# High parts of the weights on GpSimd, high parts of x and the rounding constant on ScalarE: a fused kernel of attention, token mixing and gated attention

## The chip, the cores and the metric

The kernel runs as one launch on one core of a Trainium2 chip. The metric is the device time in microseconds. The kernel before took 553.32 us (median of three runs, 553.31 to 554.25).

## The reference

Inputs are float32, apart from the token-mixing weights (`w_theta`, `w_tok_r`, `w_tok_i`, `w_ch`), which the kernel receives as float64. The data passes through three stages, 4 batches, 576 positions, 512 channels:

```python
# 1: attention, 8 heads of 64: heads 0-3 see the last 32 positions, heads 4-7 every 32nd one before
scores = scale * q @ k.T; scores = where(mask, scores, -1e9)
attn = softmax(scores); x = attn @ v                       # (B, 576, 512)
# 2: token mixing
theta = x @ w_theta
yr = einsum('ts,bsd->btd', w_tok_r, x * cos(theta))
yi = einsum('ts,bsd->btd', w_tok_i, x * sin(theta))
u = x + yr + yi
x = u + maximum(u @ w_ch, 0)
# 3: 4 experts of causal attention (q, k, v, o projections per expert), a gate picks 2 for each position
logits = x @ w_gate; out = sum over the best 2 experts of softmax gate * expert(x)
```

## The kernel before, in words

**Two halves of each number.** Every matmul of stage 2 and most of stage 3 is done on numbers split in two: a high part, rounded by writing to the type fp32r, and a low part, the number less its high part. `mm3` (lines 264 to 268) then issues three matmuls: high by high (L266), high by low (L267), low by high (L268).

**Weights.** `load64` (l. 122) brings a float64 weight in 34 pieces of 128 partitions: 8 of `w_theta` (wth, 256 columns), 18 of the token weights (wtk, 288 columns), 8 of `w_ch` (wch, 256 columns). Each piece takes a DMA of the raw words into one of eight slots (four in buffer X[1], four in X[3]; L135, issued by SyncE), a cast of the top bits on ScalarE (L139), a shift-and-or on VectorE that makes a float32 (L140), and then `split_w`: the high part by an ACTIVATE on ScalarE (L102), the low part by a subtraction on VectorE (L104; L106 for wth, where a scale comes in). A slot is free for the next raw piece once L139 and L140 of the piece in it are done.

**Stage 1** (`attn_pair`, l. 173) goes by pair of heads: scores (s, L189), maximum and exponential, sum and reciprocal (L215 to L217), the product p by it (L218: VectorE in batch 0, GpSimd in the others), the transpose of p on TensorE (tp, L221), the values (av) and a copy into X (L249, L251). The pairs of batch 1 run among the matmuls of stage 2 of batch 0: `next_pair` loads their q, k and v and calls `attn_pair`.

**Stage 2.** `split_act` (l. 254) splits x: the high part (L260) on VectorE for batch 0, on ScalarE (L258) for stage 2's output; the low part at L262. `theta` (l. 276) makes 5 tiles of theta in each of two halves of 256 columns, adds the constant MAGIC (L289, VectorE, which rounds to whole turns), takes the difference (L290), its absolute value (L291, ScalarE), and `sines` the cosine (L303, with a bias read from a tile) and the sine (L304), whose table ScalarE has to load first. `rotate` multiplies x (transposed by TensorE to xn, L312) by both (L322; L328 and L329 for the short last tile), and splits the product z: high part L332 or L334, low part L336. `tokens` runs y (L266 to L268) and adds it into X (L351), splits the sum u (L361), and `channels` makes g from it.

**The order of the work.** No order is written out: the program is built with a scheduler that simulates a timeline and decides the order of the instructions on each engine, so that a changed duration or engine moves other instructions. `issue_after` holds back a few of them. TensorE's accumulator of `th` and of the first `y` is the same pair of buffers (`acc`), so y starts when the last reader of a th tile, L290, has let it go.

Of the kernel before, what the change touches and what calls it, by code (L numbers as in the profile page):

```python
# [12 lines left out]
F32 = mybir.dt.float32  # L13
# [5 lines left out]
AF = mybir.ActivationFunctionType  # L19
ALU = mybir.AluOpType  # L20
# [3 lines left out]
B, S, DM, HD, NE = 4, 576, 512, 64, 4  # L24
# [17 lines left out]
MAGIC = 12582912.0  # L42
# [5 lines left out]
def fused_kernel(ctx: ExitStack, tc: tile.TileContext, ql, kl, vl, qs, ks, vs, wth, wtk, wch, wqk, wvg, wo, out):  # L48
    nc = tc.nc

    def f(ap):
        return ap.bitcast(F32)

    const = ctx.enter_context(tc.tile_pool(name="const", bufs=1))
# [44 lines left out]

    pha = ph1.enter_context(ExitStack())  # L100
    def split_w(hi, lo, st, scale=1.0, eng=nc.gpsimd):
        nc.scalar.activation(hi, st, AF.Copy, scale=scale)  # L102
        if scale == 1.0:
            eng.tensor_tensor(lo, st, f(hi), op=ALU.subtract)  # L104
        else:
            nc.vector.scalar_tensor_tensor(lo, st, scale, f(hi), op0=ALU.mult, op1=ALU.subtract)  # L106

    def load_split(pool, spool, src, kt, n, name):
        hi = pool.tile([128, kt, n], F32R, name=f"{name}_hi")
        lo = pool.tile([128, kt, n], F32R, name=f"{name}_lo")  # L110
        for c in range(kt):
            st = spool.tile([128, 512], F32, tag="stage", name=f"{name}_st{c}")
            nc.sync.dma_start(st[:, :n], src[:, c, :])
            split_w(hi[:, c, :], lo[:, c, :], st[:, :n])
        return hi, lo
# [6 lines left out]
    def load64(dst, src, kt, n0, n1, scale=1.0, late=False):  # L122

        hi, lo = dst
        n = n1 - n0
        for c in range(kt):  # L130
            place = X[3] if late or len(pieces) % 2 else X[1]
            raw = place.bitcast(U16)[:, len(pieces) // (1 if late else 2) % 4, :4 * n]
            pieces.append(c)
            st = X[2][:, c % 4, HALF:HALF + n]
            nc.sync.dma_start(raw[:, :4 * n - 1], src[:, c, n0:n1].bitcast(U16)[:, 1:])  # L135
            mid = raw.bitcast(U32).rearrange("p (n t) -> p n t", t=2)[:, :, 0]
            top = raw.bitcast(BF16).rearrange("p (n t) -> p n t", t=4)[:, :, 2]
            head = X[2][:, c % 4, :n]
            got = nc.scalar.copy(head.bitcast(F16).rearrange("p (n t) -> p n t", t=2)[:, :, 1], top)  # L139
            nc.vector.scalar_tensor_tensor(st.bitcast(U32), mid, 13, head.bitcast(U32), op0=ALU.logical_shift_right,  # L140
                                           op1=ALU.bitwise_or)
            split_w(hi[:, c, n0:n1], lo[:, c, n0:n1], st, scale, nc.vector)
        return got.ins
# [110 lines left out]
    def split_act(x, name):  # L254
        hi = act.tile([128, S], F32R, tag="ahi", name=f"{name}_hi")
        lo = act.tile([128, S], F32R, tag="alo", name=f"{name}_lo")
        if len(xsplit) == B:
            nc.scalar.copy(hi, x)  # L258
        else:
            nc.vector.tensor_copy(hi, x)  # L260
        eng = nc.vector if not xsplit or len(xsplit) == B and name.endswith(("0", "2")) else nc.gpsimd
        halved[name] = eng.tensor_tensor(lo, x, f(hi), op=ALU.subtract).ins  # L262
        return hi, lo

    def mm3(ps, ahi, alo, bhi, blo, first, last):
        nc.tensor.matmul(ps, ahi, bhi, start=first, stop=False)  # L266
        nc.tensor.matmul(ps, ahi, blo, start=False, stop=False)  # L267
        return nc.tensor.matmul(ps, alo, bhi, start=False, stop=last)  # L268

    def split_x(b):  # L270
        return [split_act(X[b][:, c, :], f"x{len(xsplit)}_{b}_{c}") for c in range(4)]

    sins, turns = {}, {}
    xsplit, trig, z = {}, {}, {}

    def theta(b, h):
        if h == 0:
            xsplit[b] = split_x(b)
        xs = xsplit[b]
        d0 = 256 * h  # L280
        for t in range(NT):
            w, t0 = TW[t], 128 * t
            th = ps1.tile([128, 512], F32, tag="s" if b == 0 and t % 2 else "acc", bufs=2, name=f"th_{b}_{h}_{t}")
            for c in range(4):
                turned = mm3(th[:w, :256], xs[c][0][:, t0:t0 + w], xs[c][1][:, t0:t0 + w],
                             wth_hi[:, c, d0:d0 + 256], wth_lo[:, c, d0:d0 + 256], c == 0, c == 3)
            cs = rp.tile([128, 2, 256], F32, tag="cs", name=f"cs_{b}_{h}_{t}")
            r = cs[:w, 1, :]
            nc.vector.tensor_scalar_add(r, th[:w, :256], MAGIC)  # L289
            nc.vector.scalar_tensor_tensor(r, r, MAGIC, th[:w, :256], op0=ALU.subtract, op1=ALU.subtract)  # L290
            last = nc.scalar.activation(cs[:w, 0, :], r, AF.Abs)  # L291
            trig[h, t] = cs
            if b == 0:
                sines(b, h, range(t, t + 1))
        if b > 0:
            with tc.issue_after(last.ins):
                sines(b, h, range(NT))
        return turned.ins

    def sines(b, h, tiles):  # L300
        for t in tiles:
            w, cs = TW[t], trig[h, t]
            nc.scalar.activation(cs[:w, 0, :], cs[:w, 0, :], AF.Sin, bias=halfpi[:w], scale=-TWO_PI)  # L303
            sins[b, h] = nc.scalar.activation(cs[:w, 1, :], cs[:w, 1, :], AF.Sin, scale=-TWO_PI).ins  # L304
# [69 lines left out]

    halfpi = const.tile([128, 1], F32, name="halfpi")
    nc.gpsimd.memset(halfpi, math.pi / 2)
    spark = const.tile([128, 1], F32, name="spark")

    nc.vector.memset(X[2][:, :, :HALF], 0.0)
# [26 lines left out]

    for b in range(B):
        theta(b, 0)
        if b > 0:
            next_pair(b, 0)  # L410
# [5 lines left out]
        if b > 0:  # L416
            next_pair(b, 1)
        turned = theta(b, 1)
        if b > 0:
            next_pair(b, 2)  # L420
# [372 lines left out]
```

## Time and profile before

| | |
|---|---|
| time, median of 3 | 553.32 us |
| the profiled execution | 551.97 us, span 550.1 us |
| mean granted TensorE clock | 0.986 of full speed |
| TensorE busy | 526.1 us of 550.1 |
| VectorE, ScalarE, GpSimd busy | 398.7, 316.1, 188.3 us |
| HBM traffic | 67 GB/s over the span |

The span is 1.9 us shorter than the execution's time. The profile's times run from the span's start. The stage in which the float64 weights arrive and batch 0 is worked through is the first 100 us; what follows is a repeated pattern of the other batches and then the experts.

### The profile page before, as it was taken

What the parts mean: (1) busy time and instruction counts of PE and PEld (TensorE: products, weight loads), DVE (VectorE), ACT (ScalarE), POOL (GpSimd) and SP (SyncE); (2) the same over time, 40 slices, a digit from 0 to 9 for tenths busy, and PEclk for the clock granted to TensorE, in tenths of its full rate; (3) what the DMA queues carried; (4) which work ended last, traced back from release to release, by engine and by line L of the source; (5) the groups of instructions that cost most, each with busy time, mean ns of one, the idle gap of its engine ahead of it and who ended that gap; (6) DMA issues with size and microseconds to landing.
All of it is one profiled execution on the core that took longest, in us unless ns stands there. A gap on an engine that the chain in (4) does not pass through costs nothing.

```text
span 550.1 us, 12483 instructions
## 1 busy us (share of the span) xinstructions
PE 526.1 (96%) x4536; PEld 503.4 (91%) x4536; DVE 398.7 (72%) x1222; ACT 316.1 (57%) x904; POOL 188.3 (34%) x273
## 2 busy tenths in 40 slices
PE   6898999999999999999999999989999999999987
PEld 5788899999999999999999998879989999999987
DVE  5979997676855566765456443798988898888972
ACT  5978984426453171632236321585787768767872
POOL 1000013321742114541125533264446434625451
PEclk9959999999999999999999999999999999999999
DMA  8966253460202141000100111000001001100112
GB/s 289 321 191 255 82 162 109 167 198 1 91 23 67 33 133 33 24 24 1 58 0 2 29 31 40 1 1 2 1 12 66 14 1 45 44 2 11 35 44 87
DMA packets 20389, 37.53 MB, mean 68 GB/s; under 512 B 2904, under 2 KB 12296, under 8 KB 20328
## 3 DMA queue, kind: packets, MB, share of 16 engines
q1 hardware_dynamic: 20328, 36.73, 20.5%
q8 instruction: 36, 0.59, 0.4%
q14 instruction: 25, 0.20, 0.1%
HBM read 32.01 MB, written 4.72 MB: 67 GB/s over the span
## 4 chain that ended last, share of the span: by engine, by line
PE 72%; DVE 12%; ACT 8%; DMA 4%; issue 2%; POOL 2%; SPq 0%; POOLq 0%; DVEq 0%; ACTq 0%
PE y L266 7%; PE y L268 7%; PE y L267 7%; PE s L189 4%; PE av L244 4%; PE g L266 3%; PE g L268 3%; PE g L267 3%; PE tp L221 3%; PE th L266 3%; DVE nm L604 3%; PE th L268 3%; PE th L267 3%; ACT p L615 2%; PE tp L625 2%
## 5 line engine op out<-in xcount | busy, mean ns | idle before, releaser
L266 PE MATMUL y<-wtk_hi,zhi 128*128 128x288 f32 x288 | 86.4, 302 | 1.5 <-DVE cs L290 1.1
L267 PE MATMUL y<-wtk_lo,zhi 128*128 128x288 f32 x288 | 85.6, 298 | 0.0
L268 PE MATMUL y<-wtk_hi,zlo 128*128 128x288 f32 x288 | 85.1, 296 | 0.0
L218 POOL TENSOR_TENSOR p<-p,sm 128x288 f32<-128x288 f32 (+2 forms) x36 | 22.2, 623 | 157.4 <-PE y L268 72.2
L622 POOL TENSOR_SCALAR p<-p,sm,gt 128x256 f32<-128x256 f32 (+1 forms) x64 | 45.5, 714 | 51.9 <-DVE sm L620 34.9
L615 ACT ACTIVATE p<-s,nm 128x128 f32<-128x128 f32 (+2 forms) x96 | 49.6, 518 | 15.1 <-DVE nm L604 7.8
L266 PEld LDWEIGHTS y<-wtk_hi,zhi 128*128 128x128 f32 x288 | 53.9, 188 | 2.1 <-ACT wtk_hi L102 1.2
L267 PEld LDWEIGHTS y<-wtk_lo,zhi 128*128 128x128 f32 x288 | 54.1, 188 | 0.0
L268 PEld LDWEIGHTS y<-wtk_hi,zlo 128*128 128x128 f32 x288 | 54.0, 188 | 0.1
L336 POOL TENSOR_TENSOR zlo<-cs,zhi 128x512 fp32r<-128x512 f32 (+1 forms) x30 | 36.0, 1214 | 46.6 <-DVE zhi L332 41.1
L266 PE MATMUL th<-wth_hi,x_hi 128*128 128x256 f32 (+1 forms) x160 | 47.8, 300 | 0.5 <-ACT X L251 0.5
L604 DVE TENSOR_REDUCE nm<-s 128x1 f32<-128x128 f32 (+2 forms) x96 | 44.2, 468 | 5.3 <-PE s L602 4.4
L267 PE MATMUL th<-wth_lo,x_hi 128*128 128x256 f32 (+1 forms) x160 | 45.6, 286 | 0.0
L268 PE MATMUL th<-wth_hi,x_lo 128*128 128x256 f32 (+1 forms) x160 | 45.4, 288 | 0.0
L189 PE MATMUL s<-k,q 128*108 128x54 f32 (+2 forms) x320 | 40.9, 268 | 2.6 <-DMA k<-in_kl 1.8
L189 PEld LDWEIGHTS s<-k,q 128*108 128x108 f32 (+1 forms) x320 | 39.0, 190 | 3.7 <-DMA q<-in_ql 1.7
L266 PE MATMUL pq<-x_hi,wqk_hi 128*128 128x288 f32 x128 | 39.8, 311 | 1.0 <-DVE q L550 0.9
L262 POOL TENSOR_TENSOR x_lo<-X,x_hi 128x576 fp32r<-128x576 f32 x20 | 29.3, 1466 | 30.8 <-DVE x_hi L260 24.4
L266 PE MATMUL g<-u_hi,wch_hi 128*128 128x288 f32 x128 | 38.6, 302 | 0.0
L634 DVE TENSOR_TENSOR ptlo<-tp,pthi 128x128 fp32r<-128x128 f32 (+4 forms) x80 | 37.6, 478 | 1.1 <-ACT pthi L633 0.6
L267 PE MATMUL pq<-x_lo,wqk_hi 128*128 128x288 f32 x128 | 38.0, 297 | 0.0
L268 PE MATMUL g<-u_hi,wch_lo 128*128 128x288 f32 x128 | 37.8, 295 | 0.0
(173 smaller groups left out, 1676.6 us busy)
## 6 DMA issues: line engine op xcount, KB each, us to landing
X<-in_wtk SPq DMA_DIRECT2D x18, 287.8 KB
q<-in_qs SPq DMA_DIRECT2D x8, 594.0 KB
q<-in_ql SPq DMA_DIRECT2D x8, 576.0 KB
v<-in_vl SPq DMA_DIRECT2D x24, 144.0 KB
out_t<-X SPq DMA_DIRECT2D x20, 128.0 KB
k<-in_kl SPq DMA_DIRECT2D x8, 304.0 KB
k<-in_ks SPq DMA_DIRECT2D x8, 288.0 KB
X<-in_wth SPq DMA_DIRECT2D x8, 255.8 KB
```

The source lines that it names most:

```text
L189: nc.tensor.matmul(s[:rm, i * kw:i * kw + w], qt[:, j0 + i, :], kt[:, k0:k0 + w], start=False, stop=i == n - 1)
L218: (nc.vector if b == 0 else nc.gpsimd).tensor_tensor(tiles(p), tiles(p), each(sm), op=ALU.mult)
L244: nc.tensor.matmul(av[64 * h:64 * h + 64, c0:c0 + wi], vg[:w, i, h, :], pt[:w, i, h, :wi], start=True, stop=True)
L262: halved[name] = eng.tensor_tensor(lo, x, f(hi), op=ALU.subtract).ins
L266: nc.tensor.matmul(ps, ahi, bhi, start=first, stop=False)
L267: nc.tensor.matmul(ps, ahi, blo, start=False, stop=False)
L268: return nc.tensor.matmul(ps, alo, bhi, start=False, stop=last)
L336: halved[b, h] = eng.tensor_tensor(lo, zf, f(hi), op=ALU.subtract).ins
L604: nc.vector.tensor_reduce(nm[:w, t + ci:t + ci + 1], s[:w, :c1 - c0], axis=AX.X, op=ALU.max, negate=True)
L615: nc.scalar.activation(p[:w, c0:c1], scs[ci][:w, :c1 - c0], AF.Exp, bias=nm[:w, t:t + 1], scale=1.0, accum_out=acc)
L622: eng.tensor_scalar(p[:w, :kn], p[:w, :kn], sm[:w, t:t + 1], gt[:w, t, e:e + 1], op0=ALU.mult, op1=ALU.mult)
L634: nc.vector.tensor_tensor(dst(ptlo), src, f(dst(pthi)), op=ALU.subtract)
```

## The change

Three edits. In `split_w` the high part of the 34 float64 pieces is made by a TENSOR_SCALAR on GpSimd (L103), in place of ScalarE's ACTIVATE; other callers of `split_w` keep ScalarE. In `split_act` the four high parts of x of batch 0 are made by ScalarE instead of VectorE. In `theta`, for batch 0, the ten additions of MAGIC go from VectorE to ScalarE (L293, an Identity with a bias read from a new tile `magic`, which GpSimd fills once).

```diff
@@ split_w
-        nc.scalar.activation(hi, st, AF.Copy, scale=scale)
+        if eng is nc.vector:
+            nc.gpsimd.tensor_scalar(hi, st, scale, 1.0, op0=ALU.mult, op1=ALU.mult)
+        else:
+            nc.scalar.activation(hi, st, AF.Copy, scale=scale)
@@ split_act
-        if len(xsplit) == B:
+        if len(xsplit) in (0, B):
             nc.scalar.copy(hi, x)
         else:
             nc.vector.tensor_copy(hi, x)
@@ theta
-            nc.vector.tensor_scalar_add(r, th[:w, :256], MAGIC)
+            if b == 0:
+                nc.scalar.activation(r, th[:w, :256], AF.Identity, bias=magic[:w])
+            else:
+                nc.vector.tensor_scalar_add(r, th[:w, :256], MAGIC)
@@ constants
+    magic = const.tile([128, 1], F32, name="magic")
+    nc.gpsimd.memset(magic, MAGIC)
```

In the changed kernel the lines from L102 on stand 3 higher, and those behind L289 6 higher (L140 is L143, L104 is L107, L217 is L220, L290 is L296, L303 is L309, L336 is L342). The scheduler's order differs up to the second theta half of batch 1; from there on TensorE's order is the same.

SyncE's issues, around the loads of batch 1's first two pairs (`X` with the slots' numbers is a raw piece of wtk, `q_1_1` and `k_1_1` are the second pair's inputs). Before:

```order
L166 DMA v_1_0_2_987<-in_vl 96x384
L135 DMA X1_62<-in_wtk 128x1151
L135 DMA X3_64<-in_wtk 128x1151
L135 DMA X1_62<-in_wtk 128x1151
L135 DMA X3_64<-in_wtk 128x1151
L161 DMA q_1_1_1075<-in_ql 128x1152
```

And now:

```order
L169 DMA v_1_0_2_989<-in_vl 96x384
L164 DMA q_1_1_1077<-in_ql 128x1152
L165 DMA k_1_1_1078<-in_kl 128x608
L138 DMA X1_62<-in_wtk 128x1151
L138 DMA X3_64<-in_wtk 128x1151
L138 DMA X1_62<-in_wtk 128x1151
```

The ninth piece of wtk (the first `X1` row behind `v_1_0_2`) and those that follow it stand behind `q_1_1` and `k_1_1` now.

ScalarE's work up to the first sine of batch 0 (`cs_0_0_0` is the first tile of the first half, `cs_0_0_1` the second). Before:

```order
L139 CAST X2_63<-X3_64 128x288
L102 ACTIVATE wtk_hi_112<-X2_63 128x288 x2
L139 CAST X2_63<-X1_62 128x288
L102 ACTIVATE wtk_hi_112<-X2_63 128x288 x3
L291 ACTIVATE cs_0_0_0_630<-cs_0_0_0_630 128x256
L303 ACT_TABLE_LOAD
```

And now:

```order
L293 ACTIVATE cs_0_0_0_632<-th_0_0_0_619,magic_108 128x256
L293 ACTIVATE cs_0_0_1_651<-th_0_0_1_638,magic_108 128x256
L293 ACTIVATE cs_0_0_2_670<-th_0_0_2_657,magic_108 128x256
L142 CAST X2_63<-X1_62 128x288
L297 ACTIVATE cs_0_0_0_632<-cs_0_0_0_632 128x256
L293 ACTIVATE cs_0_0_3_689<-th_0_0_3_676,magic_108 128x256
L297 ACTIVATE cs_0_0_1_651<-cs_0_0_1_651 128x256
L309 ACT_TABLE_LOAD
```

The cast of the ninth piece of wtk stands ahead of the table load in both. Behind it stood three high parts and one absolute value; now there are two absolute values and one addition of MAGIC.

VectorE's work ahead of the first reciprocal of batch 1's attention (`sm_1_0_0`). Before:

```order
L140 SCALAR_TENSOR_TENSOR X2_63<-X3_64,X2_63 128x256
L104 TENSOR_TENSOR wtk_lo_113<-X2_63,wtk_hi_112 128x288
L104 TENSOR_TENSOR wch_lo_115<-X2_63,wch_hi_114 128x256
L361 TENSOR_TENSOR u_0_0_lo_1288<-X0_61,u_0_0_hi_1287 128x288
L361 TENSOR_TENSOR u_0_1_lo_1292<-X0_61,u_0_1_hi_1291 128x288
L211 TENSOR_TENSOR p_1_0_2_1039<-s_1_0_2_1032,mx_1_0_2_1037 128x288
L217 RECIPROCAL sm_1_0_0_995<-sm_1_0_0_995 128x3
L216 TENSOR_SCALAR sm_1_0_1_1017<-sm_1_0_1_1017 128x3
```

And now:

```order
L143 SCALAR_TENSOR_TENSOR X2_63<-X3_64,X2_63 128x256
L342 TENSOR_TENSOR zlo_0_1_4_931<-cs_0_1_4_889,zhi_0_1_4_930 128x256
L218 TENSOR_REDUCE sm_1_0_1_1019<-p_1_0_1_1020 128x3
L367 TENSOR_TENSOR u_0_0_lo_1290<-X0_61,u_0_0_hi_1289 128x288
L367 TENSOR_TENSOR u_0_1_lo_1294<-X0_61,u_0_1_hi_1293 128x288
L107 TENSOR_TENSOR wch_lo_117<-X2_63,wch_hi_116 128x256
L143 SCALAR_TENSOR_TENSOR X2_63<-X3_64,X2_63 128x256
L220 RECIPROCAL sm_1_0_0_997<-sm_1_0_0_997 128x3
```

The last `L143` row ahead of the reciprocal is the fourth piece of wch; before, that reciprocal came behind the second. From the release of the first accumulator by `L290` (tile `cs_0_1_2`) to this reciprocal VectorE had 44 instructions and has 47, one of them 288 columns wide more and two of 256.

## Rows read from the trace of the kernel before

**Rows 1.** Page part 1, busy time and share of the span by engine:

```profile
PE 526.1 (96%) x4536; PEld 503.4 (91%) x4536; DVE 398.7 (72%) x1222; ACT 316.1 (57%) x904; POOL 188.3 (34%) x273
```

**Rows 2.** Timeline of PE, its four stops (start, duration, instruction, idle before):

```profile
36.06 0.58 PE L266 MATMUL th<-wth_hi,x_hi 128*128 128x256 f32 x1 [0.49 <-ACT X L251]
...
54.11 0.41 PE L312 MATMUL xn<-ident,X 128*128 128x128 f32 x2 [1.65 <-DVE cs L329]
...
57.93 0.37 PE L266 MATMUL y<-wtk_hi,zhi 128*128 128x288 f32 x1 [1.10 <-DVE cs L290]
...
76.78 0.43 PE L221 MATMUL tp<-ident,p 128*96 128x128 f32 x2 [0.71 <-POOL p L218]
```

**Rows 3.** Windows: stretch, length, busy PE, PEld, DVE, ACT, POOL, clock, DMA, GB/s:

```profile
24.00:28.00 4.00, 2.11 (x25) 1.27 (x23) 4.00 (x16) 4.00 (x25) 0.00 (x0) 0.80 0.68 227
28.00:36.00 8.00, 6.97 (x84) 5.71 (x83) 5.29 (x18) 5.28 (x17) 0.00 (x0) 0.50 0.50 150
...
40.00:44.00 4.00, 4.00 (x36) 4.00 (x35) 3.72 (x11) 2.49 (x8) 0.00 (x0) 1.00 1.07 339
52.00:58.00 6.00, 3.25 (x27) 2.63 (x24) 5.94 (x16) 5.25 (x16) 0.00 (x0) 1.00 0.08 13
58.00:77.00 19.00, 18.29 (x142) 17.81 (x143) 18.94 (x51) 16.97 (x49) 1.40 (x1) 1.00 0.48 148
```

**Rows 4.** Groups by form on ACT: count, busy and mean ns, idle before:

```profile
L102 ACT ACTIVATE wtk_hi<-X 128x288 fp32r<-128x288 f32 x18 | 7.4, 434 | 0.2 <-DVE X L140 0.2
L258 ACT CAST x_hi<-X 128x576 fp32r<-128x576 f32 x16 | 10.0, 672 | 0.2 <-PE th L267 0.2
L303 ACT ACTIVATE cs<-cs,halfpi 128x256 f32<-128x256 f32 x32 | 16.0, 499 | 0.1
```

**Rows 5.** Groups by form on DVE:

```profile
L289 DVE TENSOR_SCALAR cs<-th 128x256 f32<-128x256 f32 x32 | 13.3, 420 | 7.2 <-PE th L268 6.7 <-POOL zlo L336 0.4
L260 DVE CAST x_hi<-X 128x576 fp32r<-128x576 f32 x16 | 9.1, 580 | 2.5 <-ACT X L251 2.3
```

**Rows 6.** Group by form on POOL:

```profile
L555 POOL TENSOR_SCALAR k<-k 64x288 fp32r<-64x288 f32 x32 | 14.5, 453 | 16.2 <-ACT k L553 14.5
```

**Rows 7.** Timeline of DVE: its first wtk piece, and two back-to-back low parts:

```profile
37.21 1.56 DVE L140 SCALAR_TENSOR_TENSOR X<-X,X 128x288 uint32<-128x288 uint32 x4
...
60.99 0.81 DVE L104 TENSOR_TENSOR wtk_lo<-X,wtk_hi 128x288 fp32r<-128x288 f32 x2
```

**Rows 8.** Timeline of ACT from the ninth wtk piece to the first sine:

```profile
42.84 0.53 ACT L139 CAST X<-X 128x288 f16<-128x288 bf16 x1 [1.51 <-DMA X<-in_wtk]
43.23 1.11 ACT L102 ACTIVATE wtk_hi<-X 128x288 fp32r<-128x288 f32 x3
...
46.43 0.40 ACT L304 ACTIVATE cs<-cs 128x256 f32<-128x256 f32 x1
```

**Rows 9.** Page part 6, DMA issues of SyncE, count and KB each:

```profile
q<-in_ql SPq DMA_DIRECT2D x8, 576.0 KB
...
k<-in_kl SPq DMA_DIRECT2D x8, 304.0 KB
```

**Rows 10.** Timeline of DVE, the first reciprocal of batch 1:

```profile
74.99 0.16 DVE L217 RECIPROCAL sm<-sm 128x3 f32<-128x3 f32 x1
```

**Rows 11.** Timeline of DVE and POOL where both work, and where DVE works alone:

```profile
75.12 0.41 DVE L140 SCALAR_TENSOR_TENSOR X<-X,X 128x256 uint32<-128x256 uint32 x1
...
77.86 0.67 POOL L218 TENSOR_TENSOR p<-p,sm 128x288 f32<-128x288 f32 x1 [1.13 <-DVE sm L217]
77.98 0.83 DVE L140 SCALAR_TENSOR_TENSOR X<-X,X 128x256 uint32<-128x256 uint32 x1
...
403.04 0.33 DVE L622 TENSOR_SCALAR p<-p,sm,gt 128x128 f32<-128x128 f32 x1
...
518.65 0.43 POOL L555 TENSOR_SCALAR k<-k 64x288 fp32r<-64x288 f32 x1 [0.32 <-ACT k L553]
518.65 0.51 DVE L622 TENSOR_SCALAR p<-p,sm,gt 128x128 f32<-128x128 f32 x1
```

## The prediction

> **What bounds the kernel now.** I read the page's shares first, then TensorE's timeline for its stops, then a table by stretch, and last the rows of the engines named in the stops. TensorE is busy for 96% of the span [rows 1], so the change can only gain what TensorE still waits for, and it can lose whatever makes it wait anew. All three edits touch the weights, x and theta of batch 0, so they lie in the first 77 us. There TensorE stops four times for one of these engines [rows 2]: 0.49 us at 36.06 (for the last copy of attention on ScalarE), 1.65 at 54.11 and 1.10 at 57.93 (both for VectorE), 0.71 at 76.78 (for a product on GpSimd, whose reciprocal VectorE made at 74.99 [rows 10]). From 58 to 77 it runs otherwise without a gap, 18.29 of 19 us. So the later stops add up to some 3.5 us, the most that an edit in this stretch can return, apart from a slow clock: from 28 to 36 TensorE is granted 0.50 of its clock (1.2 GHz), from 40 on all of it (2.4 GHz) [rows 3].
>
> What the reader is to see in the table by stretch is VectorE: 5.94 of 6 us busy from 52 to 58, 18.94 of 19 from 58 to 77, 3.72 of 4 from 40 to 44 [rows 3]. From its first wtk piece at 37.21 [rows 7] to the reciprocal's end at 75.15 it works 36.6 of 37.9 us. It makes the sines' arguments, the low parts and the reciprocal in one queue. GpSimd is empty there, but for the product p that starts at 75.33 and is 1.40 us busy in the window. So relieving VectorE would pay, relieving ScalarE alone would not.
>
> **The change part by part.** Removed from VectorE: 4 x high parts at 0.580 and 10 additions at 0.420 [rows 5], with two of the ten shorter: about 6 us by these means. Back to back an instruction takes less than its own duration: two 288-wide low parts in 0.81 [rows 7], a pitch of 0.37 with the ramp taken off; in the same way I use 0.34 for 256 columns and 0.60 for 512. Removed from ScalarE: 34 high parts, 18 of them at 0.434 [rows 4]. Added to ScalarE: 4 casts of x at 0.672 and 10 additions, which I price by the form with a bias from a tile, 0.499, pitch 0.42 [rows 4]. Added to GpSimd: 34 TENSOR_SCALARs; the nearest row is 0.453 for 64 by 288 [rows 6]. That is 34 x 0.45 = 15.3 us on an engine with nothing else to do, in a chain that was cast, shift, high, low and still is: by throughput it costs nothing. Four terms follow in time.
>
> First, theta starts sooner. VectorE has its last p of attention behind fewer low parts of wth, about three of 0.34 less, and TensorE, at half clock, gives on most of that: 0.85, start 35.2.
>
> Second, the last x high part stands on ScalarE behind four wtk casts that it used to precede on VectorE, and its low part goes ahead of VectorE's first wtk piece: 37.21 becomes 38.0, a loss of 0.8 that eats what the first term gave.
>
> Third, the ninth wtk piece. In the order of SyncE's issues `q_1_1` and `k_1_1` now stand ahead of it: 576 + 304 KB [rows 9]. At 339 GB/s [rows 3] that is 2.6 us; I take 2.4, an estimate, since the ends of such loads run side by side. The queue is 0.85 earlier by the first term, so the piece lands 1.5 later than its 42.84 [rows 8], at 44.4; ScalarE already waits 1.51 for that DMA before, so nothing hides the delay. Behind it ScalarE had 1.11 us of high parts [rows 8] and one absolute value before the table load; now it has two absolute values and an addition. So the first sine's end, 46.83 before [rows 8], goes to about 47.9: 1.5 of the landing, less some 0.4 of the shorter queue. From there ScalarE's chain of five additions, absolute values and sines is the one that VectorE waits for, but VectorE has no additions any more. I get the first accumulator's release at 56.1, y at 56.2 instead of 57.93: 1.7 gained there.
>
> Fourth, from this release to the reciprocal. Before, that was 57.78 to 75.15, 17.4 us for 44 instructions; now there are 47, one of 288 columns and two of 256 more: 0.37 + 2 x 0.34 = 1.05, so 18.4. To this comes a price that no row shows in this form: 13 of the high parts (9 wtk, 4 wch) run on GpSimd beside VectorE's two-input instructions. At 77.98 an L140 took 0.83 where the same instruction took 0.41 at 75.12, and the GpSimd product began at 77.86: VectorE was held 0.42. The single-input TENSOR_SCALAR of GpSimd, which the new instruction is, went with 0.51 for an L622 against 0.33 undisturbed, a hold of 0.18 [rows 11]. The bounds are thus zero (GpSimd's instruction waits in place of VectorE's) and 13 x 0.45 = 5.9; I take 0.2 each, by the row of the same form, 2.6. The reciprocal ends at 56.1 + 18.4 + 2.6 = 77.1, which is 2.0 later than 75.15. On GpSimd the high part of the fourth wch piece (0.41) stands ahead of the product p, which then takes 0.67 [rows 11]: with 0.17 to the start on GpSimd and 0.1 to TensorE the transposes start at 78.35 instead of 76.78, 1.57 later. A score matmul (0.8) that used to run ahead of them is left for behind: 2.4 in all.
>
> The gain of 1.7 at y is inside that sum: TensorE comes to the transposes 1.7 sooner and waits there longer, some 4 us in place of 0.71. Behind them the order is the same and TensorE has no wait in this stage, so the loss stays. The profiled execution's 551.97 (its span and 1.9 around it) goes to 554.4, and the median of the runs, 553.32, to 553.3 + 2.4 = 555.7.
>
> The Trainium skill has a rule for this place: "Advanced Engine Details and Errata", section VectorE Performance Modes, Mode Summary, says that the second SBUF port is shared with GpSimd, so that instructions of VectorE in the two-port mode and GpSimd's block each other. By it alone a two-input subtraction, which needs no such mode, would not be held and the fourth term would be 2.6 smaller. The held L140 [rows 11] speaks against reading it so narrowly. In the same Trainium skill "GPSIMD Engine Reference", section 1. Specifications, counts instructions with two SBUF inputs to the contention as well; the trace agrees.
>
> **The rivals.** *No hold, order alone.* GpSimd's high parts wait instead of VectorE. For it: a 288-wide high part has no reader in a hurry. Against it: both rows of [rows 11]. The reciprocal ends at 74.5, the transposes follow 1.35 later (waits, high part, p) at 75.85 where they were at 76.78, a gain of 0.9 that the score matmul behind takes back: -0.1, 553.2.
>
> *VectorE's relief goes through*, on the other side: faster. If the ninth piece lands by 42.8 (the loads ahead of it are taken in side by side) and there is no hold, VectorE's stretch is its work alone: from 38.0, 33.9 us of work (36.6 less ten additions at 0.37, plus the 1.05 of moved work) and 1.2 idle, reciprocal 73.1, transposes 74.55, so -2.2 + 0.8 = -1.4: 551.9. It decides from a reciprocal before 73.4.
>
> *Held to the bound, with a slow clock.* TensorE waits over 4 us at the transposes. From 24 to 28 it was busy 2.11 of 4 us and the granted clock fell to 0.80, then 0.50 [rows 3]; from 52 to 58, busy 3.25 of 6, it stayed at 1.00. A fall here would double its matmuls for some time: with a hold of up to 0.4 each (2.6 more) or a few us at 0.50, 1.5 to 3 us above the forecast, 557 to 558.7.
>
> *The clock stays up earlier.* If TensorE's gaps around 26 close, the 14 us at 0.50 would shorten. ScalarE's changed queue there is neither fuller nor emptier; and VectorE, which sets y, would take little of it: 1.7 off the forecast, 554.
>
> That the change does not do what it says can be left out: the new instructions stand in the order.
>
> **How the numbers follow.** Forecast 0.40, with its own range 554.4 to 557.0 (a hold of 0.1 to 0.3 each, and 0.85 either way in the first term); of the earlier clock I count nothing apart. Held with a slow clock 0.18, no hold 0.20, relief goes through 0.22. What can be told from no change is 0.2%, 1.1 us: slower has 0.40 + 0.18 = 0.58, same 0.20, faster 0.22. The range takes in the relief's 551.9 and the slow clock's upper end: 551.5 to 558.6.
>
> **What would show it.** Right, step by step: theta's first matmul near 35.2; VectorE's first wtk L143 near 38.0; the ninth piece's cast at 44 or later, behind an idle for its DMA; y near 56.2; VectorE's L143 and L107 beside GpSimd's L103 longer by some 0.2 than alone; the reciprocal near 77; a stop of about 4 us before the transposes at 78.35. Wrong: two-input instructions of VectorE with the same pitch under L103, the reciprocal before 74.5, or a stop at the transposes under a microsecond; or a change of time that lies beyond 100 us, where the order is the same.

## The result and the profile after

The changed kernel takes 557.03 us (median of 20 runs, 554.57 to 560.66), the kernel before on the same chips 553.45 (551.05 to 558.23, 20 runs). The ratio is 1.0054, 95% interval 1.0031 to 1.0076: slower, by 1.7 to 4.2 us. The runs of every kernel here, the one before too, fall into two groups some 4 us apart, the upper one with a lower granted clock over the span, and in either group the change is 2.4 us slower (medians 555.75 against 553.31, and 559.6 against 557.24), while the ratio also counts that 8 of its 20 runs, against 3 of 20, lie in the upper group. Below, the ratios and the profiles are compared, not single medians. A profile is one execution.

The profiled execution has a span of 553.0 us, 2.9 over that of before. TensorE's stops in it, as in [rows 2] (start, duration, instruction, idle before):

```profile
35.42 0.55 PE L269 MATMUL th<-wth_hi,x_hi 128*128 128x256 f32 x1 [0.59 <-ACT X L254]
44.80 0.33 PE L269 MATMUL th<-wth_hi,x_hi 128*64 128x256 f32 x1 [0.77 <-DVE cs L296]
54.18 0.33 PE L269 MATMUL th<-wth_hi,x_hi 128*64 128x256 f32 x1 [0.49 <-DVE cs L296]
...
56.55 0.38 PE L269 MATMUL y<-wtk_hi,zhi 128*128 128x288 f32 x1
...
77.62 0.88 PE L224 MATMUL tp<-ident,p 128*96 128x128 f32 x3 [2.49 <-POOL p L221]
78.54 0.44 PE L270 MATMUL y<-wtk_lo,zhi 128*128 128x288 f32 x1
```

The two stops for VectorE at 54.11 and 57.93 are gone or small and y starts at 56.55, 1.4 us sooner; but the transposes now wait 2.49 us instead of 0.71, and the matmuls behind them take 0.44 where such matmuls took 0.29. Behind the stop of before, one such matmul and the stretch around it (columns as in [rows 3]):

```profile
78.08 0.29 PE L267 MATMUL y<-wtk_lo,zhi 128*128 128x288 f32 x1
...
78.00:80.00 2.00, 2.00 (x17) 2.00 (x17) 2.00 (x6) 2.00 (x11) 0.53 (x1) 1.00 0.29 110
```

And the table by stretch now:

```profile
58.00:77.00 19.00, 16.55 (x124) 15.59 (x123) 18.61 (x46) 15.23 (x42) 9.43 (x13) 1.00 0.43 123
...
76.00:78.00 2.00, 0.38 (x2) 0.37 (x3) 2.00 (x7) 0.69 (x2) 1.21 (x2) 0.86 0.90 315
78.00:80.00 2.00, 2.00 (x11) 1.99 (x10) 2.00 (x8) 0.10 (x1) 1.04 (x2) 0.50 0.80 297
80.00:82.00 2.00, 2.00 (x14) 2.00 (x14) 1.93 (x5) 1.91 (x8) 1.96 (x3) 0.79 0.09 36
```

After the stop the clock is 0.50 (1.2 GHz), and on its way back to 2.4 GHz between 80 and 82; before, it stayed at 1.00 behind the stop of 0.71. GpSimd, the fifth busy column, went from 1.40 to 9.43 us between 58 and 77, and VectorE is as full as it was: 18.61 against 18.94. Counted matmul by matmul from the last one back, TensorE is 2.97 us later than before at 84.6 us, and from 107 us on, where the order is the same, 2.75 to 3.1 later all the way to the end. So in this execution the whole loss is made in the stretch of the weights.

The chain that makes the transposes late (VectorE, ScalarE and GpSimd in one list, in order of time):

```profile
37.95 2.01 DVE L143 SCALAR_TENSOR_TENSOR X<-X,X 128x288 uint32<-128x288 uint32 x4
44.41 0.52 ACT L142 CAST X<-X 128x288 f16<-128x288 bf16 x1 [1.77 <-DMA X<-in_wtk]
47.63 0.40 ACT L310 ACTIVATE cs<-cs 128x256 f32<-128x256 f32 x1
55.88 0.41 DVE L296 SCALAR_TENSOR_TENSOR cs<-cs,th 128x256 f32<-128x256 f32 x1
58.62 1.27 DVE L107 TENSOR_TENSOR wtk_lo<-X,wtk_hi 128x288 fp32r<-128x288 f32 x2
64.03 4.62 POOL L103 TENSOR_SCALAR wtk_hi<-X 128x288 fp32r<-128x288 f32 x3 [0.72 <-DVE X L143]
66.55 0.44 DVE L107 TENSOR_TENSOR wtk_lo<-X,wtk_hi 128x288 fp32r<-128x288 f32 x1
68.30 0.67 DVE L107 TENSOR_TENSOR wtk_lo<-X,wtk_hi 128x288 fp32r<-128x288 f32 x1 [0.33 <-POOL wtk_hi L103]
76.20 0.16 DVE L220 RECIPROCAL sm<-sm 128x3 f32<-128x3 f32 x1
76.36 0.58 POOL L103 TENSOR_SCALAR wch_hi<-X 128x256 fp32r<-128x256 f32 x1 [1.58 <-DVE sm L220]
76.91 0.67 POOL L221 TENSOR_TENSOR p<-p,sm 128x288 f32<-128x288 f32 x1
```

The reciprocal ends at 76.36, 1.21 later than in [rows 10], and the fourth wch high part stands between it and the product. GpSimd and VectorE slow each other, but not in one way. At 58.62 two low parts take 1.27 where two took 0.81 [rows 7], and the low part at 68.30 both waits for a high part and lasts 0.67 instead of 0.44: there VectorE pays. The three high parts at 64.03 take 1.54 each, while VectorE's instructions beside them keep their time (0.44 at 66.55): there GpSimd waits instead.

### The profile page after: what moved, and what is told of

It reads as the page before. It is cut to its first block, busy times and chain, and to the rows that moved or that the text cites. A ratio compares the mean times of both kernels' runs of the same rounds, so it can differ in the third digit from the quotient of the medians.

```text
span 553.0 us, 12499 instructions
## 1 busy us (share of the span) xinstructions
PE 529.2 (96%) x4536; PEld 506.0 (92%) x4536; DVE 397.1 (72%) x1208; ACT 311.6 (56%) x884; POOL 213.2 (39%) x308
## 4 chain that ended last, share of the span: by engine, by line
PE 68%; DVE 11%; ACT 4%; issue 1%; POOL 1%; DMA 1%; POOLq 0%; DVEq 0%; ACTq 0%
PE y L269 6%; PE y L271 6%; PE y L270 6%; PE s L192 3%; PE g L269 3%; PE g L271 3%; PE g L270 3%; PE av L247 3%; PE th L269 3%; PE th L271 3%; PE th L270 3%; PE tp L633 2%; DVE nm L612 2%; PE tp L224 2%; PE o L589 2%; PE s L607 2%
## 5 line engine op out<-in xcount | busy, mean ns | idle before, releaser
L342 POOL TENSOR_TENSOR zlo<-cs,zhi 128x512 fp32r<-128x512 f32 (+1 forms) x30 | 36.0, 1212 | 47.0 <-DVE zhi L338 41.5
L192 PEld LDWEIGHTS s<-k,q 128*108 128x108 f32 (+1 forms) x320 | 40.3, 195 | 2.5 <-issue 2.5
```

Source lines behind the costliest of these rows:

```text
L192: nc.tensor.matmul(s[:rm, i * kw:i * kw + w], qt[:, j0 + i, :], kt[:, k0:k0 + w], start=False, stop=i == n - 1)
L342: halved[b, h] = eng.tensor_tensor(lo, zf, f(hi), op=ALU.subtract).ins
```

## The experiments

Each was timed in five rounds beside the kernel before (12 runs, 6 of the first one), except the one with the added tail, which ran once. "Late" is TensorE's lateness against the kernel before in the profiled execution, matmul by matmul, where the order is the same again. Theta's start differs between executions, so the part of it that was there by then is given too. Of edits that also collect names, only the line that acts is shown.

**The high parts on GpSimd alone.** The edit is the change's first hunk:

```diff
-        nc.scalar.activation(hi, st, AF.Copy, scale=scale)
+        if eng is nc.vector:
+            nc.gpsimd.tensor_scalar(hi, st, scale, 1.0, op0=ALU.mult, op1=ALU.mult)
+        else:
+            nc.scalar.activation(hi, st, AF.Copy, scale=scale)
```

> Only the high parts of the 34 float64 pieces go to GpSimd. Theory (the GpSimd route is what costs: VectorE's two-input instructions are held and the high parts come late): VectorE's queue from the accumulator's release to the first reciprocal of batch 1 has 42 instructions here instead of 44, and some 9 high parts at 0.12 us each beside it, so the transposes come within 0.5 us of where they were, but GpSimd's own lateness at the low parts shows; time +0.5 to +1.5 us over the kernel before. Rival (the order of the loads is the cause, which the x edit moves): no change, -0.5 to +0.5. Rival (the edits each cost a third): +1.

Measured: 562.0 us, ratio 1.0112 (1.0069 to 1.0156), some 6 us slower, twice the whole change. All theories sized it too small; the sign is that of the GpSimd route. TensorE's stops, some of them new:

```profile
48.21 0.33 PE L269 MATMUL th<-wth_hi,x_hi 128*64 128x256 f32 x1 [1.77 <-DVE cs L293]
59.34 0.28 PE L188 MATMUL s<-mask_l,twice 128*128 128x288 bf16 x1 [0.88 <-DVE cs L293]
66.80 0.40 PE L269 MATMUL y<-wtk_hi,zhi 128*128 128x288 f32 x1 [1.26 <-DVE cs L293]
84.45 0.40 PE L269 MATMUL y<-wtk_hi,zhi 128*128 128x288 f32 x1 [1.48 <-DVE X L354]
```

All of these wait for VectorE, which still has its additions and casts here. TensorE is 7.3 us late from 158 to 341 us, 1.7 of it at theta's start. By the ratios the other two edits give back some 3 us of that in the whole change, though neither gains anything alone, as the next two runs show.

**The high parts of x alone.**

```diff
-        if len(xsplit) == B:
+        if len(xsplit) in (0, B):
```

> Only the four high parts of x of batch 0 go to ScalarE. In this order, too, q_1_1 and k_1_1 stand ahead of the ninth wtk piece. Theory (GpSimd route): the ninth piece lands some 1.5 us later, but VectorE has slack from the four casts; time 0 to +1 us. Rival (order of the loads): nearly the whole loss appears here, +2 to +3 us, with a stop of TensorE over 1.5 us at the transposes or at y.

Measured: 555.72, ratio 1.0023 (0.9989 to 1.0057). Not to be told from no change or +1; the rival's +2 to +3 is only at the interval's end, and the transposes show no stop. But the profiled execution is 3.4 us late from 158 us on, 1.2 of it at theta's start, with a stop at xn that was 1.65 before and a new one at a y:

```profile
56.91 0.30 PE L312 MATMUL xn<-ident,X 128*128 128x128 f32 x1 [2.23 <-DVE cs L329]
80.27 0.40 PE L266 MATMUL y<-wtk_hi,zhi 128*128 128x288 f32 x1 [1.04 <-DVE X L351]
```

So this run doesn't settle whether the order of the loads costs anything; what it costs in the whole change is asked by the run with the two loads moved back.

**The additions of MAGIC alone.**

```diff
-            nc.vector.tensor_scalar_add(r, th[:w, :256], MAGIC)
+            if b == 0:
+                nc.scalar.activation(r, th[:w, :256], AF.Identity, bias=magic[:w])
+            else:
+                nc.vector.tensor_scalar_add(r, th[:w, :256], MAGIC)
```

> Only the ten additions of MAGIC go to ScalarE. VectorE loses ten instructions of about 0.37 us before y, so y starts some 1.5 us earlier; the scheduler puts 36 more matmuls (4.8 us) ahead of the first transposes of batch 1. Theory (GpSimd route costs, the relief of VectorE is real): the stops at y and at the transposes shrink, time -1 to -2.5 us. Rival (each edit costs a third): +1. Rival (ScalarE's longer queue makes the sines late): stop at xn grows, 0 to +1.

Measured: 556.32, ratio 1.0012 (0.9979 to 1.0045): the forecast gain of 1 to 2.5 us is outside the interval but for its edge, and in the profile TensorE is only 0.1 to 0.2 us sooner from 158 to 341 us. The stops at y and at the transposes are gone, the one at xn is smaller, and others have come, where TensorE waits for VectorE at the scores of batch 1:

```profile
55.70 0.41 PE L315 MATMUL xn<-ident,X 128*128 128x128 f32 x2 [0.63 <-DVE cs L332]
71.35 0.30 PE L185 MATMUL s<-mask_l,twice 128*128 128x288 bf16 x1 [0.56 <-DVE p L211]
75.60 0.30 PE L185 MATMUL s<-mask_l,twice 128*128 128x288 bf16 x1 [1.15 <-DVE p L211]
```

**Both ScalarE edits without the GpSimd route.** The last two diffs together.

> Both ScalarE edits, the high parts of the weights left on ScalarE: the change without the GpSimd route. The ninth wtk piece comes late as in the change (cast at 44 or later); the scheduler puts 50 more matmuls (6.6 us) ahead of the first transposes. Theory: without high parts on GpSimd the loss goes; TensorE does not wait over 1 us at the transposes and keeps its full clock there, time -2 to 0 us against the kernel before. Rival (order of the loads): +1.5 to +3 us as in the whole change.

Measured: 554.2, ratio 0.999 (0.9961 to 1.0019). Without the high parts on GpSimd most of the loss is gone: the interval, which leaves up to 1.1 us, does not overlap that of the whole change, and TensorE is 1.4 to 1.5 us late from 158 us on (0.4 at theta's start) instead of 3.0. That GpSimd's part is the cause rests on this pair, and on the first run. The order of the loads is the same late one here. But the scheduler's order differs too (50 matmuls), and no run keeps the change's order without GpSimd, so how much of GpSimd's part is the two engines' slowing each other, and how much the order, is not shown. A stop of 2.49 us is there too, at a y, without a fall of the clock behind it (1.00 up to 100 us), so my expectation that it would vanish was right for the transposes only:

```profile
76.43 0.40 PE L266 MATMUL y<-wtk_hi,zhi 128*128 128x288 f32 x1 [2.49 <-DVE X L354]
```

**The hold by itself.** The kernel before with a tail behind the outputs:

```diff
+    def stream(kind):            # 12 back to back, 128x288, on VectorE
+        ...
+    def high():                  # 12 back to back, 128x288, on GpSimd
+        ...
+    for kind in ("sub", "shift", "one", "psum"):
+        stream(kind)             # alone, behind the GpSimd work
+        high()
+        stream(kind)             # beside high()
```

> The kernel before with a tail that adds work of no use to the output: 12 back-to-back VectorE instructions of 128x288 of four kinds (two SBUF inputs subtracted; shift-and-or of two SBUF inputs; one SBUF input; one PSUM and one SBUF input), each kind alone and beside 12 of GpSimd's single-input TENSOR_SCALARs, which also run alone once. Theory (the prediction's: VectorE is held): alone 0.37 us a step for the two-input kinds, beside GpSimd 0.45 to 0.6, the PSUM kind unchanged; GpSimd 0.43 to 0.6. Rival (GpSimd waits in place of VectorE, as its 1.54 us a piece at 64 us in the changed kernel suggests): VectorE keeps 0.37 to 0.40, GpSimd's steps grow to 0.8 us or more while two-input instructions run, and stay near 0.43 beside the PSUM kind.

GpSimd alone, then the subtraction alone and beside it, the shift, the one-input kind, and the kind with a PSUM input (start, time of the 12, engine and line):

```profile
553.05 4.99 POOL L749 TENSOR_SCALAR X<-X 128x288 fp32r<-128x288 f32 x12 [7.45 <-DVE X L730]
558.75 4.51 DVE L738 TENSOR_TENSOR X<-X 128x288 fp32r<-128x288 f32 x12
563.91 7.05 POOL L749 TENSOR_SCALAR X<-X 128x288 fp32r<-128x288 f32 x12 [5.87 <-DVE X L752]
564.76 6.88 DVE L738 TENSOR_TENSOR X<-X 128x288 fp32r<-128x288 f32 x12
572.60 4.51 DVE L740 SCALAR_TENSOR_TENSOR X<-X 128x288 uint32<-128x288 uint32 x12
578.61 6.88 DVE L740 SCALAR_TENSOR_TENSOR X<-X 128x288 uint32<-128x288 uint32 x12
586.46 2.72 DVE L743 TENSOR_SCALAR X<-X 128x288 f32<-128x288 f32 x12
590.66 5.09 DVE L743 TENSOR_SCALAR X<-X 128x288 f32<-128x288 f32 x12
597.09 4.47 DVE L745 TENSOR_TENSOR X<-hold,X 128x288 f32<-128x288 f32 x12
602.45 4.87 POOL L749 TENSOR_SCALAR X<-X 128x288 fp32r<-128x288 f32 x12 [7.07 <-DVE X L752]
603.07 4.47 DVE L745 TENSOR_TENSOR X<-hold,X 128x288 f32<-128x288 f32 x12
```

VectorE's two-input instructions go from 4.51 to 6.88 us for 12, 0.20 each: the price that the prediction took. GpSimd pays nearly as much, 4.99 to 7.05, 0.17 each. With an input in PSUM neither pays. So the theory's ranges hold (0.57 a step on VectorE, 0.59 on GpSimd), and the rival's, VectorE at 0.40 or less and GpSimd at 0.8 or more, do not: in back-to-back streams each engine slows the other. The Trainium skill ("GPSIMD Engine Reference", section 1. Specifications) counts instructions of VectorE with two SBUF inputs among those that contend; the tail agrees. The Trainium skill's "Advanced Engine Details and Errata" (VectorE Performance Modes, Mode Summary) names only the two-port mode, by which the subtraction would have kept its 4.51; the measurement decides against that reading.

**The eight high parts of wch on ScalarE.**

```diff
-        if eng is nc.vector:
+        if eng is nc.vector and len(pieces) <= 26:
```

> The change, but the eight high parts of wch stay on ScalarE; VectorE's 47 instructions ahead of the reciprocal are the same. Theory (VectorE's queue ahead of the reciprocal sets the transposes, GpSimd's high part ahead of the product adds 0.55): the transposes come 0.4 to 0.8 us sooner than the 77.62 of the change; time 0.5 to 1 us under the change, still 1.5 to 2.5 over the kernel before. Rival (all of the loss is the high parts' lateness at wtk): no change against the change. Rival (the clock after the stop is the whole loss): back to the kernel before only if the stop falls under 1 us, which it does not here.

Measured: 558.19, ratio 1.0041 (1.0009 to 1.0073), 0.7 us under the change by the ratios, inside the theory's 0.5 to 1, though the intervals overlap. In the profile the stop is 1.79 instead of 2.49, the product standing alone on GpSimd; the clock fell to 0.50 behind it here too. The theory asked for transposes 0.4 to 0.8 sooner than 77.62; they start at 77.72, but theta started at 36.23 in this execution, 0.81 later, so against theta they are 0.71 sooner.

```profile
76.65 0.17 DVE L220 RECIPROCAL sm<-sm 128x3 f32<-128x3 f32 x1
...
77.00 0.67 POOL L221 TENSOR_TENSOR p<-p,sm 128x288 f32<-128x288 f32 x1 [7.55 <-DVE sm L220]
...
77.72 0.53 PE L224 MATMUL tp<-ident,p 128*96 128x128 f32 x3 [1.79 <-POOL p L221]
```

**The pieces of wch held behind the reciprocal.** The change, with wch's instructions ordered behind batch 1's first reciprocal on VectorE and product on GpSimd:

```diff
-            with tc.issue_after(sins[0, 1]):
+            with tc.issue_after(sins[0, 1]), tc.issue_after(recips[1, 0, 0]), tc.issue_after(prods[1, 0, 0]):
```

> The change, but the pieces of wch wait for the first reciprocal and product of batch 1 (an ordering edge on VectorE and GpSimd alone): VectorE has 41 instructions instead of 47 ahead of that reciprocal. Theory (its queue sets the transposes): six instructions at 0.34 and GpSimd's 0.55 less, so the reciprocal near 74.2 and the transposes near 75.1 instead of 77.62; the stop of 2.49 shrinks under 0.5 us, the clock does not fall, and the offset of TensorE behind it goes from +2.97 to between -0.5 and +0.7; time -0.5 to +0.7 us against the kernel before, if wch still arrives in time for g. Rival (GpSimd's high parts of wtk and wth cost as much): +1.5 to +3.

Measured: 554.8, ratio 1.0006 (0.9976 to 1.0035): by the ratio most of the loss is gone, but its interval overlaps that of the change. In the profile TensorE is 2.7 us late from 158 to 341 us, 1.3 of it at theta's start; the change is 3.0 late with theta 0.6 sooner than before. So behind theta 1.4 us are left of 3.6. Against theta's start (37.32 in this execution, 1.90 later) the reciprocal is 2.4 us sooner, more than the 2.0 forecast. But the stop is 1.11, not under 0.5:

```profile
75.73 0.17 DVE L221 RECIPROCAL sm<-sm 128x3 f32<-128x3 f32 x1
75.82 1.07 DVE L143 SCALAR_TENSOR_TENSOR X<-X,X 128x256 uint32<-128x256 uint32 x3
...
76.08 2.04 POOL L222 TENSOR_TENSOR p<-p,sm 128x288 f32<-128x288 f32 x1 [5.50 <-PE y L273]
...
78.18 0.53 PE L226 MATMUL tp<-ident,p 128*96 128x128 f32 x3 [1.11 <-POOL p L222]
```

The held pieces now stand right behind the reciprocal, and three of VectorE's two-input instructions run while GpSimd makes the product, which takes 2.04 instead of 0.67. The clock stays at 1.00.

**The same, with that product on VectorE.**

```diff
-            (nc.vector if b == 0 else nc.gpsimd).tensor_tensor(tiles(p), tiles(p), each(sm), op=ALU.mult)
+            (nc.vector if b == 0 or (b, pair, g) == (1, 0, 0) else nc.gpsimd).tensor_tensor(tiles(p), tiles(p), each(sm), op=ALU.mult)
```

> As with the pieces of wch held behind the first reciprocal, and that first product of batch 1 made on VectorE instead of GpSimd, where it took 2.04 us beside three of VectorE's two-input instructions. Theory (GpSimd is starved there): the product takes 0.45 on VectorE, five rows behind the reciprocal; the scheduler places the transposes 21 matmuls (2.8 us) later, and no stop over 0.3 us is left at them; 0.8 to 1.5 us under the version with wch held alone, so 0 to +0.8 against the kernel before. Rival (the remaining loss is the high parts of wtk, at y and the sines): no change against the version with wch held.

Measured: 556.81, ratio 1.0022 (0.9984 to 1.0059). The time does not tell; the expected 0.8 to 1.5 us under the version above isn't shown. In the profile no stop above 0.1 us is left between 63 and 104. TensorE is 1.0 us late from 158 to 341 us, where the change is 3.0 late, and 0.9 of that were there at theta's start; but it then lost 3 us again behind 341, where the mean clock from 340 to 400 was 0.94. So in this execution nearly nothing of the change's loss behind theta is left up to 341 us, though the high parts of wth and wtk are still on GpSimd: what is lost there goes with the wch pieces ahead of the reciprocal and with the product beside them (the transposes also stand 21 matmuls later here).

**The two loads behind wtk again.**

```diff
+        with tc.issue_after(wdma[19]) if (b, pair) == (1, 1) else nullcontext():
+            nc.sync.dma_start(qt, (ql if local else qs)[b, pj])
+            nc.sync.dma_start(kt[:, :kn], (kl if local else ks)[b, pj])
```

> The change, with the two loads q_1_1 and k_1_1 held on the queue behind the twelfth piece of wtk, as in the kernel before. Theory (the loads cost 1.5 us of landing, of which VectorE's full queue takes some): the ninth piece's cast comes 1.5 us sooner against theta's start, at 7.5 us behind it instead of 9.0; VectorE has 42 instructions instead of 47 ahead of the reciprocal, which comes 1.5 to 2 us sooner; the stop at the transposes goes from 2.49 to under 1.2 and the clock does not fall: time 1.3 to 2.5 us under the change, +0.5 to +1.7 against the kernel before. Rival (VectorE's queue is full there anyway, so the landing is hidden): no change, +2.5 to +3.

Measured: 558.16, ratio 1.005 (1.0015 to 1.0085): no gain, as the rival has it. The cast came at 42.63, 1.78 sooner, as the theory said, with theta at 35.51. But the first absolute value then waited for VectorE's difference, and y started only 0.05 sooner than in the change:

```profile
44.87 0.42 ACT L298 ACTIVATE cs<-cs 128x256 f32<-128x256 f32 x1 [0.65 <-DVE cs L297]
...
56.50 0.38 PE L270 MATMUL y<-wtk_hi,zhi 128*128 128x288 f32 x1
```

The reciprocal, with 42 instructions ahead of it instead of 47, came at 74.40, 1.80 sooner, and the transposes ran at 75.96 without a wait. Then TensorE waited 2.74 us for the next accumulator:

```profile
77.12 1.28 DVE L143 SCALAR_TENSOR_TENSOR X<-X,X 128x256 uint32<-128x256 uint32 x3
...
78.69 0.81 DVE L358 TENSOR_TENSOR X<-y,X 128x288 f32<-128x288 f32 x2
...
79.19 0.40 PE L270 MATMUL y<-wtk_hi,zhi 128*128 128x288 f32 x1 [2.74 <-DVE X L358]
```

VectorE's addition that releases y stands behind the wch pieces there, as the reciprocal did in the change. The stop moved within one full queue; the clock stayed at 1.00 behind it.

**MAGIC on ScalarE with wch held; and that with the product on VectorE.** The edits of the two versions above on the kernel before, with the high parts on ScalarE.

> Only the additions of MAGIC on ScalarE, and the pieces of wch held behind the first reciprocal and product of batch 1; a version meant to beat both. Theory: y starts some 1.5 us earlier as with the additions alone, and the 46 instructions (instead of 55) ahead of the reciprocal bring it forward by 3 us, so that no stop is left at the transposes and none later: -1 to -2.5 us against the kernel before. Rival (stops later, at the g matmuls, which need wch): 0 to +1.

Measured: 554.74, ratio 0.9996 (0.9967 to 1.0025).

> Additions of MAGIC on ScalarE, wch held behind the first reciprocal and product, that product on VectorE: the candidate for a version that beats both. Theory: TensorE's gaps behind theta's start were 1.66 us with wch held, against 3.50 in the kernel before, and the last of them at the scores (0.57, 0.30) shrink a little more: -1 to -2 us against the kernel before. Rival (what the stops give back is lost in the clock or in the first 20 us): within 0.2% of it.

Measured: 553.69, ratio 0.9983 (0.9951 to 1.0015). Neither beats the kernel before by more than the measurement can tell, though TensorE's gaps from theta to 115 us, added up from the trace, are 1.7 and 1.9 us against 3.5. The "within 0.2%" of the second version's rival fits both.

## Why the prediction was right

The direction and the place came out as forecast: VectorE's queue ahead of the reciprocal, and GpSimd beside it, made the transposes late. The range holds the time, but it reached from 551.5 to 558.6 and took in a gain as well, so that says little. Of the steps, some agree by luck:

- *First term*: theta at 35.2; it was 35.42. That is luck as far as the runs show: four other executions with the change's order up to there started theta at 35.51, 36.23, 36.92 and 37.32, and four with the order of before at 36.06, 36.09, 36.75 and 38.46. A gain of 0.85 can't be told from that scatter.
- *Second*: VectorE's first wtk piece at 38.0; it was 37.95.
- *Third*: the ninth piece's cast at 44.4, the first sine's end at about 47.9, y at 56.2; they were 44.41, 48.03 and 56.55. Moving the loads back moved the cast by 1.78, so the two loads are its cause. But the path from the cast to y was not the one that the term has: with the cast 1.78 sooner the first sine ended 0.25 sooner and y started 0.05 sooner, because the first absolute value waited for VectorE's difference, which ended at 44.84 there and at 44.75 in the change. VectorE's queue of wtk pieces sets that, and the times agree by luck.
- *Fourth*: 18.4 us of VectorE's work and 2.6 of holds, reciprocal's end at 77.1. From the release at 56.29 to 76.36 it was 20.1, so holds and waits for high parts came to 1.7, not 2.6: by the trace some 1.2 of longer instructions and 0.4 of idle. The price of 0.20 was right for back-to-back work; 13 times 0.20 was too much, because at 64.03 three high parts waited and VectorE beside them did not. That is what the prediction named as a sign of being wrong, and it holds for these three.
- *The transposes* at 78.35; they were at 77.62, by the smaller hold, and the stop was 2.49, not about 4. That is 0.84 later than before instead of 1.57, plus the group of score matmuls behind them, 0.7.
- *The slow clock*, held as a rival with 0.18, came beside the forecast instead of in place of it: from 77.6 to about 81 the clock was at 0.50, worth about 1.4 by the table above (half of 2.0 us, and 0.21 of the 2.0 behind them). 0.84 + 0.7 + 1.4 = 2.9: the loss in the profile, where the forecast's 2.4 came from 1.6 + 0.8.

So two sizes were off and their errors cancelled in part: the delay that the forecast adds up came to 1.5 of its 2.4 us, and the slow clock, which it left out, gave the rest. That the time came so near is luck. The 36.6 us read as VectorE's work from 37.21 to 75.15 are 37.2 in the window; only the relief rival rests on them. "No hold" fell with the added tail as a rule, though not for the three high parts at 64.03; "relief goes through" did not happen, because VectorE's work per piece stayed and only moved. The fourth rival, an earlier end of the slow clock before theta, did not come: from 28 to 36 it was 0.50 again. What stays open is why the clock fell after the stop of 2.49 at the transposes and not after the equal stop at y without the GpSimd route, nor after the 2.74 with the loads moved. Open too is how GpSimd's part divides between the slowing and the order.

## What to carry to other kernels

Work moved to an idle engine isn't free if the full engine and it slow each other: price it at what both lose together (back to back 0.20 on VectorE and 0.17 on GpSimd for each 128x288 piece, less in the kernel), and look which instruction stands behind it in the full engine's queue. When a full queue sets the end, undoing one delay moves the stop to the next reader of that queue (transposes, y, scores); the order within the queue has to be changed along with the work. VectorE's instructions with an input in PSUM are the ones to leave beside GpSimd: in the tail they cost neither engine anything.

## What the runs showed of the hardware

GpSimd can be starved beyond an even share: three single-input high parts took 4.62 us at 64.03 in the change, and one product 2.04 beside three L143 (0.67 alone), while VectorE's instructions beside the three kept their time; back-to-back streams of both slowed each other nearly evenly. A one-input VectorE instruction of 128x288 float32 in SBUF, at 0.23 a step the quickest alone, loses as much as the two-input kinds beside GpSimd (2.72 to 5.09 us for 12). The version with MAGIC on ScalarE and wch held has the order of before up to theta, yet started theta 2.4 us later in its profiled execution, so profiles are best compared from a common point such as theta's start.
